# One first block of 512 tokens, another order from the third block on, and a new place for the first chunk of w_in

## The chip, the cores and the metric

The kernel runs on one core of one Trainium2 chip. The metric is the device time of one execution in microseconds. TensorE (PE) multiplies matrices, VectorE (DVE) and ScalarE (ACT) do elementwise work, GpSimd (POOL) some additions, and the queue of SyncE (SP) issues the transfers between HBM and the on-chip memory.

## What is computed

Attention with a bounded window over 4 x 768 tokens and 8 heads of 64, then two feed-forward networks:

```python
# per chunk of 32 queries: 8 memory keys, 16 keys to the left, the chunk, 8 to the right
scores = scale * (q_c @ k_full.T)
a = exp(scores - max(scores)); a = a / (sum(a) + 1e-9)
x = a @ v_full                                   # tokens x 512
h = x @ w_in                                     # 512 x 2048
g = maximum(h, 0) + alpha * minimum(h, 0)
y = g @ w_out                                    # 2048 x 512
out = ((y @ w_a) * (y @ w_b)) @ w_out2           # 512 x 1536, 512 x 1536, 1536 x 512
```

The inputs are 64-bit floats; the kernel reads them as pairs of 32-bit words.

## The kernel before

Attention works in 24 units of 128 tokens. A unit turns k and q (PE, lines 716 and 705), evacuates them, forms the scores (line 740; for the first eight units PE adds the mask, line 731), takes their maximum (DVE, line 756), the exponentials (ACT, line 766) and the normalisation (line 782), turns the probabilities P (PE, line 792) and multiplies them with v (line 806) into x32.

Products are exact to more than 16 bits by splitting: each operand is scaled by a power of two and split into a high f16 part (`split_hi`, ACT, line 347) and a low one (`split_lo`, DVE, line 351), and a product is three matmuls, high x high, high x low, low x high (`gemm3`, lines 910 to 912). The scale needs the largest value of a whole operand: a transpose on PE (line 310) and a chain of small DVE steps (lines 315 to 326).

Weights come as words. Eight chunks of w_in and eight of w_out are turned into 32-bit floats on ACT and DVE (lines 531 to 560), scaled and split. The whole of w_in has one scale, so none of its chunks can be split before all eight are in. w_in's words lie in places that are free at the start: its first chunk in xhl (later the split x), the next three in ghl, the last four where w_out's split form will be. `raw` has three places for the words of w_out and, later, of the second network's weights (`wa`, `wb`, `w3`; 18 chunks, split and spilled to HBM).

Tokens go through the first network in blocks. `first = [2, 2]` makes two blocks of 256 tokens; five of 512 follow. For each block `gemm1` forms g for 16 slices of w_in, and `gemm2` forms y for 4 slices. The two first blocks share xhl and ghl: both have their `gemm1` before the `gemm2`. From 680 us on the second network runs in six passes of 512 tokens (`second`), with the products built from seven part products; for the last pass the operands of the output product are made by `operands`: four additions over quarter blocks (`sums`, line 367, on POOL or DVE) and the splits, once the scale of the whole pass is known.

All this is written as operations with costs in microseconds (`dve`, `act`, `pe`, ...), ranks and dependencies. `Schedule.emit` plays them through on a model of the engines and issues whichever can start first; the order that results is fixed in each engine's queue. So the costs don't change what an instruction takes on the chip, only its place in the queue.

Of the kernel before, what the change touches and what calls it, by code (L numbers as in the profile page):

```python
# [13 lines left out]
ALU = mybir.AluOpType  # L14
# [157 lines left out]


def dve(n, rate=1.04, pointers=0):
    return 0.07 + 0.06 * pointers + n * rate / 1000


def act(n, pointers=0):
    return 0.06 + 0.09 * pointers + n * 0.833 / 1000

# [10 lines left out]
def tile_attention_moe_moe2(  # L191
# [15 lines left out]
    nc = tc.nc  # L207
# [11 lines left out]
    KF2 = DF2 // P  # L219
    TB = 512  # L220
    EARLY = 8
    CW = 256
    CR = 64
# [80 lines left out]
    def scale(amax, s, inv, reads, writes, rank=-2000, after=()):  # L304


        ps = Buf(mm_slots)

        def across():
            nc.tensor.transpose(out=ps.tile[:, :P], in_=amax().to_broadcast([P, P]), identity=ident)  # L310

        m = Buf(m_slots)

        def largest():
            nc.vector.tensor_reduce(out=m.tile, in_=ps.tile[:, :P], axis=AX.X, op=ALU.max)
# [12 lines left out]
        sd.op("PE", pe(P, 2), -9000, across, reads, [(ps, 0)])  # L328
        sd.op("DVE", dve(P), rank, largest, [(ps, 0)], [(m, 0)])
        sd.op("DVE", 0.07, rank, power, [], [(m, 0)])  # L330
        sd.op("DVE", 0.07, rank, inverse, [(m, 0)], [(m, 1)])
        last = [(m, 2)] if after else writes
        sd.op("DVE", 0.09, rank, itself, [(m, 1)], last)
        for i, fn in enumerate(after):
            sd.op("DVE", 0.07, rank, fn, [(m, 2 + i)], writes if i == len(after) - 1 else [(m, 3 + i)])

# [143 lines left out]
    def raw_tile(c):  # L480
        if c < 4:
            t = (in_g if c else in_x).tile.rearrange("p x k t -> p (x k t)")
            c = max(0, c - 1)
# [21 lines left out]
    def chunk(nm, c, w, kt, cw, rank, load_rank):  # L505
# [84 lines left out]
        if nm != "w1":  # L590
            sd.op("ACT", act(n, 2), rank, sizes, [fk], [rk, (key + "am", 0)])
            scale(
                lambda: am, s, inv, [(key + "am", 0)], [(key + "s", 0), (f"inv_{nm}{c}", 0)],
                rank=rank - 0.3, after=[after],
            )
# [65 lines left out]
    def attention(iu, b, u, x32, part, am, rank):  # L661
# [166 lines left out]
        sd.op(  # L828
            "PE", 0.3 + 4 * pe(KW, 4) + (0.35 if early else 0.0), prank, scores,
            [(qT, 0), (kT, 0), (kT, 1)], [(ps, 0)],  # L830
# [6 lines left out]
        sd.op("ACT", 8 * act(KW, 2) + 0.3, rank, exps, [(sm, "m")] + [(ps, 0)] * early, [(sm, 0)])  # L837
        sd.op("DVE", 0.07, rank, sums, [(sm, 0)], [(sm, 2)])
        sd.op("DVE", 0.09, rank, part_of, [], [(sm, 2)])
        for o in range(2):  # L840
            sd.op(
                None, {"DVE": dve(n), "ACT": 4 * act(KW, 1) + 0.15}, rank, lambda e, o=o: norm(e, o),
                [(sm, 2), (sm, 0)], [(sm, ("n", o))],
            )
            sd.op("PE", 4 * pe(P, 2), prank, lambda o=o: p_turn(o), [(sm, ("n", o))], [(pp, o)])
            sd.op(None, either(512), rank, lambda e, o=o: p_evac(e, o), [(pp, o)], [(pT, o)])
        sd.op("PE", 0.3 + 8 * pe(64, 4), prank, values, [(vw, 0), (pT, 0), (pT, 1)], [(px, 0)], holds=[x32])
        sd.op(None, either(512), rank, x_evac, [(px, 0)], [(x32, part)])
# [17 lines left out]
    def x_block(jb, x32, xhl, c0, rank):  # L866
# [12 lines left out]
        sd.op(  # L879
            "DVE", 0.1, rank, largest, [(x32, ("am", p0 + i)) for i in range(nu)], [(f"amx{jb}", 0)]  # L880
        )

        after = [
            lambda: nc.vector.tensor_tensor(out=s, in0=s, in1=ral, op=ALU.mult),

            lambda: nc.vector.tensor_tensor(out=iy, in0=inv, in1=iy0, op=ALU.mult),
        ]
# [72 lines left out]
    def gemm2(jb, m, ghl, c0, n, iy, rank):  # L960
# [25 lines left out]
        for i in range(4):  # L986
# [7 lines left out]
            "DVE", 0.07, rank - 1000, evac_scale,  # L994
            [(f"sx{jb}", 0)] + [(f"inv_w2{2 * m + i}", 0) for i in range(2)], [("iym", jb, m)],
        )
# [38 lines left out]
    for c in range(NR):  # L1035
        chunk("w2", c, w_out, KF1, CR, 5 + c, 4.1 + 0.5 * c)
    shared = Buf(x32_slots), Buf(xhl_slots), Buf(ghl_slots)
    place = []
    for jb in range(NB):
        if jb < len(first):  # L1040
            place.append((*shared, blocks[jb][0] * P, (-6, -3.2, -3.1, -3.0)[jb], 5 + 0.1 * jb, 8 + 0.1 * jb))
        else:
            b = jb - len(first) + 2
            ar = 9 if b == 2 else (b - 1) * 10 + 4
            place.append((Buf(x32_slots), Buf(xhl_slots), Buf(ghl_slots), 0, ar, b * 10 + 5, b * 10 + 8))
    for jb, (x32, xhl, ghl, c0, ar, r1, r2) in enumerate(place):
        n = blocks[jb][1] * P
        iy = x_block(jb, x32, xhl, c0, ar)
# [4 lines left out]
    for i, (nm, w) in enumerate((("wa", w_a), ("wb", w_b), ("w3", w_o2))):  # L1053
        for c in range(NJ):
            chunk(nm, c, w, 0, 0, 1000 + c, 1000 + c)


# [116 lines left out]

    def operands(r, b, h, s, reads, cost):

        o = Buf(s32_slots)
        unit = lambda: b.tile
        others = lambda: o.tile

        sd.op("POOL", 0.0, r, lambda: None, reads, [(h, "held")], holds=[h])
        sums(
# [16 lines left out]
    def second(jb, r):  # L1199
# [39 lines left out]

        sd.op("DVE", 0.1, r, largest_y, [(f"amy{jb}", kk) for kk in range(KK)], [(f"amy1{jb}", 0)], late=3.0)  # L1240
        after = [
# [12 lines left out]

        sd.op("DVE", 0.1, r, largest, [("amp", jb, j) for j in js], [(f"amp1{jb}", 0)], late=0.0 if last_ else 3.0)
        after = [
# [123 lines left out]
```

## Time and profile before

| | us |
|---|---|
| median of 3 runs | 1192.36 (1191.29 to 1195.16) |
| the profiled execution's own time | 1191.92 |
| its span, first to last instruction | 1190.2 |
| PE busy | 1126.7 (95%) |
| DVE busy | 868.6 (73%) |
| ACT busy | 604.7 (51%) |
| POOL busy | 226.5 (19%) |

A matmul's row gives its start and a modelled end, and the next begins before that end; so the distance of starts is what a matmul costs. [...] An idle time in brackets is that of the engine before the row, with what ended it.

### The profile page before, as it was taken

The numbers are of one execution on the slowest core, as the hardware profiler recorded it, in microseconds if no ns is written. First come the engines' busy times: TensorE is split into PE (matmuls) and PEld (weight loads), VectorE is DVE, ScalarE is ACT, GpSimd is POOL, SyncE is SP. The second block draws the span as 40 slices with busy tenths as digits, with TensorE's granted clock in tenths as the row PEclk, the third lists the DMA queues.
The fourth block names the chain that finished last, engine by engine and source line by source line (L and its number), as shares of the span: only waits on it lengthen the run. The fifth ranks groups of instructions, "written<-read, shape, count | busy, mean of one in ns | idle before, by whom it ended". The sixth has DMA issues, their size and how long they took to land.

```text
span 1190.2 us, 23137 instructions
## 1 busy us (share of the span) xinstructions
PE 1126.7 (95%) x9304; PEld 811.2 (68%) x9304; DVE 868.6 (73%) x1533; ACT 604.7 (51%) x1326; POOL 226.5 (19%) x293
## 2 busy tenths in 40 slices
PE   4399999999999999999999999999999999999988
PEld 3278886555445554444444588888888888888877
DVE  6989998987998799335243187886867958858881
ACT  4689778975886698246253032433424423324340
POOL 1000012111112212100300010242433414234130
PEclk9589999999999999899999999999999999999999
DMA  9935664647635633530103052512513514315101
GB/s 263 258 81 139 154 191 127 186 132 219 200 103 167 194 127 106 179 140 32 50 10 133 27 190 90 188 66 94 191 54 112 173 37 156 130 52 187 63 36 37
DMA packets 162523, 150.93 MB, mean 127 GB/s; under 512 B 104032, under 2 KB 139888, under 8 KB 162416
## 3 DMA queue, kind: packets, MB, share of 16 engines
q1 hardware_dynamic: 162416, 149.45, 41.5%
q8 instruction: 73, 1.20, 0.4%
q14 instruction: 34, 0.28, 0.1%
HBM read 120.33 MB, written 29.10 MB: 126 GB/s over the span
## 4 chain that ended last, share of the span: by engine, by line
PE 74%; DVE 13%; ACT 6%; DMA 3%; SPq 2%; issue 2%; ACTq 0%; DVEq 0%
PE mm L910 23%; PE mm L912 23%; PE mm L911 23%; ACT sm L766 2%; PE pair L792 2%; DVE ghl L942 1%; DVE g L933 1%; DVE w L553 1%; PE mm L806 1%; DMA qt<-in_q_dram 1%; SPq L688 1%; DVE nm L756 1%; DVE w L560 1%; ACT sp L347 1%; ACT t L930 1%
## 5 line engine op out<-in xcount | busy, mean ns | idle before, releaser
L912 PE MATMUL mm<-xhl,w 128*128 128x512 f16 (+1 forms) x448 | 157.3, 351 | 1.9 <-DVE w L553 1.9
L910 PE MATMUL mm<-xhl,w 128*128 128x512 f16 (+1 forms) x448 | 157.6, 352 | 0.3 <-ACT t L930 0.2
L912 PE MATMUL mm<-ghl,w 128*128 128x512 f16 (+1 forms) x448 | 156.9, 350 | 0.9 <-DVE w L351 0.9
L911 PE MATMUL mm<-xhl,w 128*128 128x512 f16 (+1 forms) x448 | 157.4, 351 | 0.3 <-DVE xhl L351 0.3
L910 PE MATMUL mm<-ghl,w 128*128 128x512 f16 (+1 forms) x448 | 157.2, 351 | 0.0
L911 PE MATMUL mm<-ghl,w 128*128 128x512 f16 (+1 forms) x448 | 156.9, 350 | 0.0
L910 PE MATMUL mm<-units,w1b 128*128 128x256 f16 x560 | 153.4, 274 | 0.0
L911 PE MATMUL mm<-units,w1b 128*128 128x256 f16 x560 | 153.4, 274 | 0.0
L912 PE MATMUL mm<-units,w1b 128*128 128x256 f16 x560 | 153.3, 274 | 0.0
L912 PEld LDWEIGHTS <-w 128*128 128x128 f16 x896 | 88.2, 98 | 83.5 <-DVE w L553 2.2
L910 PEld LDWEIGHTS <-w 128*128 128x128 f16 x896 | 88.5, 99 | 75.5 <-issue 0.8
L911 PEld LDWEIGHTS <-w 128*128 128x128 f16 x896 | 88.3, 99 | 73.5 <-issue 1.7
L910 PE MATMUL mm<-w2b,w1b 128*128 128x256 f16 x504 | 137.4, 273 | 0.1
L912 PE MATMUL mm<-w2b,w1b 128*128 128x256 f16 x504 | 137.4, 273 | 0.0
L911 PE MATMUL mm<-w2b,w1b 128*128 128x256 f16 x504 | 137.4, 273 | 0.0
L910 PEld LDWEIGHTS <-w1b 128*128 128x128 f16 x1064 | 104.4, 98 | 13.0 <-DMA w1b<-wb_d 0.5
L911 PEld LDWEIGHTS <-w1b 128*128 128x128 f16 x1064 | 104.4, 98 | 12.7
L912 PEld LDWEIGHTS <-w1b 128*128 128x128 f16 x1064 | 104.4, 98 | 12.2
L367 POOL TENSOR_TENSOR raw<-w 128x256 f32<-128x256 f32 x18 | 16.1, 893 | 409.7 <-ACT raw L568 248.8
L933 DVE SCALAR_TENSOR_TENSOR g<-t,columns,g 128x512 f32<-128x512 f32 (+1 forms) x112 | 75.8, 683 | 24.3 <-ACT t L930 24.2
L942 DVE TENSOR_TENSOR ghl<-g,ghl 128x512 f16<-128x512 f32 (+1 forms) x112 | 70.8, 638 | 23.8 <-ACT ghl L939 23.4
L927 ACT ACTIVATE g<-mm 128x512 f32<-128x512 f32 (+1 forms) x112 | 60.5, 547 | 50.5 <-PE mm L912 48.4
(293 smaller groups left out, 2403.5 us busy)
## 6 DMA issues: line engine op xcount, KB each, us to landing
w1b<-wa_d SPq DMA_DIRECT2D x26, 896.0 KB
w1b<-wb_d SPq DMA_DIRECT2D x26, 896.0 KB
raw<-in_moe_w_out_dram SPq DMA_DIRECT2D x8, 1024.0 KB
kw<-in_k_dram SPq DMA_DIRECT2D x40, 176.0 KB
vw<-in_v_dram SPq DMA_DIRECT2D x40, 176.0 KB
qt<-in_q_dram SPq DMA_DIRECT2D x24, 256.0 KB
raw<-in_moe_w_a_dram SPq DMA_DIRECT2D x12, 512.0 KB
raw<-in_moe_w_b_dram SPq DMA_DIRECT2D x12, 512.0 KB
```

The lines of the kernel that those rows point to most:

```text
L347: nc.scalar.activation(out=hi, in_=src, func=ACTF.Copy, scale=s)
L367: (nc.vector if e == "DVE" else nc.gpsimd).tensor_tensor(out=out_()[:, i], in0=x()[:, a], in1=y()[:, b], op=op)
L553: nc.vector.scalar_tensor_tensor(out=f, in0=lo, scalar=29, in1=f, op0=ALU.logical_shift_right, op1=ALU.bitwise_or)
L560: nc.vector.scalar_tensor_tensor(out=lo if nm == "w1" else f, in0=hi, scalar=KEEP, in1=f, op0=ALU.bitwise_and, op1=ALU.bitwise_or)
L766: nc.scalar.activation(out=sm.tile[:, o, g], in_=scored()[:, o, g], func=ACTF.Exp, bias=stat["nm"][:, i : i + 1], scale=1.0, accum_out=sta ...
L792: nc.tensor.transpose(out=heads(pp, P)[:KW, o, g], in_=sm.tile[:, o, g], identity=ident)
L910: nc.tensor.matmul(out=ps, lhsT=lh, rhs=rh, start=first and i == 0, stop=False)
L911: nc.tensor.matmul(out=ps, lhsT=lh, rhs=rl, start=False, stop=False)
L912: nc.tensor.matmul(out=ps, lhsT=ll, rhs=rh, start=False, stop=last and i == n - 1)
L927: nc.scalar.activation(out=g.tile[:, :n], in_=ps.tile[:, :n], func=ACTF.Relu, scale=E1)
L933: nc.vector.scalar_tensor_tensor(out=g.tile[:, :n], in0=t2.tile[:, :n], scalar=nal[:, m : m + 1], in1=g.tile[:, :n], op0=ALU.mult, op1=ALU ...
L942: nc.vector.tensor_tensor(out=ghl.tile[:, 1, m, d], in0=g.tile[:, :n], in1=ghl.tile[:, 0, m, d], op=ALU.subtract,)
```

## The change

One block of 512 tokens stands first instead of two of 256, so there are six blocks of 512, and the first product needs four units of attention. The costs that the planner uses become a table, `took`: `SHORT` holds the values as they were, `FULL` longer ones; from the third block on, and for the second network's weight chunks, `FULL` holds. w_in's first chunk goes to a place of `raw`, where w_out's third chunk then has to wait for it; w_out's loads get a later rank. The scale of x no longer waits for that of w_in (a factor `iy` is its own operation now), and 18 copies of a scale's reciprocal fall away. In the last pass the additions of `operands` may start as soon as a product and its size are there (`ready`) instead of after the scale, the first two operands have their additions in places of their own, and the places of the split operands are dealt in another order.

```diff
+SHORT = dict(
+    dve=0.07, act=0.06, rate=0.833, tiny=0.07, itself=0.09, part=0.09, largest=0.1,
+    exp=0.357, scaled=0.267, scores=1.16, values=2.02,
+)
+FULL = dict(
+    dve=0.15, act=0.17, rate=0.85, tiny=0.15, itself=0.16, part=0.2, largest=0.2,
+    exp=0.57, scaled=0.42, scores=0.9, values=1.15,
+)
+took = dict(SHORT)
 def dve(n, rate=1.04, pointers=0):
-    return 0.07 + 0.06 * pointers + n * rate / 1000
+    return took["dve"] + 0.06 * pointers + n * rate / 1000
...
-    in_x, in_g = Buf(xhl_slots), Buf(ghl_slots)
+    in_x, in_g = Buf(raw_slots), Buf(ghl_slots)
...
-    first = [2, 2]
+    first = [4]
...
         scale(
-            lambda: am1, s, inv, [(f"amx{jb}", 0), ("alpha", 0), ("s_w1", 0)], [(f"sx{jb}", 0)], after=after
+            lambda: am1, s, inv, [(f"amx{jb}", 0), ("alpha", 0)], [(f"sx{jb}", 0)], after=after
+        )
+        sd.op(
+            "DVE", took["tiny"], rank, lambda: nc.vector.tensor_tensor(out=iy, in0=inv, in1=iy0, op=ALU.mult),
+            [(f"sx{jb}", 0), ("s_w1", 0)], [(f"iy{jb}", 0)],
         )
...
-        chunk("w2", c, w_out, KF1, CR, 5 + c, 4.1 + 0.5 * c)
+        chunk("w2", c, w_out, KF1, CR, 5 + c, 6.1 + 0.5 * c)
...
+        took.update(SHORT if jb < EXACT else FULL)
...
-    def operands(r, b, h, s, reads, cost):
-        o = Buf(s32_slots)
+    def operands(r, b, h, s, reads, cost, ready=None, slots_=None):
+        o = Buf(slots_ or s32_slots)
...
-        sd.op("POOL", 0.0, r, lambda: None, reads, [(h, "held")], holds=[h])
+        sd.op("POOL", 0.0, r, lambda: None, reads if ready is None else ready, [(h, "held")], holds=[h])
...
-        pu = {j: Buf((ring_slots if i < 4 else yu_slots) if last_ else pu_slots) for i, j in enumerate(js)}
+        pu = {j: Buf((yu_slots if i < 2 else ring_slots) if last_ else pu_slots) for i, j in enumerate(js)}
         for j in js:
-            operands(r, ps[j], pu[j], lambda j=j: spj[:, j : j + 1], [(f"sp{jb}", 0), (ps[j], 0)], cost)
+            operands(
+                r, ps[j], pu[j], lambda j=j: spj[:, j : j + 1], [(f"sp{jb}", 0), (ps[j], 0)], cost,
+                [(ps[j], 0), ("amp", jb, j)] if last_ else None,
+                p32_slots if last_ and j in list(js)[:2] else None,
+            )
```

Lines of the changed kernel stand 12 to 23 further down: 716 becomes 728, 705 becomes 717, 740 becomes 752, 792 becomes 804, 806 becomes 818, 310 becomes 324, 351 becomes 365, 367 becomes 381, 910 becomes 925.

On PE, at the start, the queue before has unit 2's scores, the transposes for the scales of w_in and of x, unit 3's q, and then the first product:

```order
L740 MATMUL pair<-kT,qT 64x96 x16
L310 MATMUL mm<-ident,columns 128x128 x2
L705 MATMUL mm<-ident,qt 128x128 x4
L910 LDWEIGHTS w_94
L910 MATMUL mm<-xhl,w_94 128x256
```

Behind the same scores of unit 2 the changed queue goes on with attention. After w_in's scale come unit 3's q, unit 2's P, unit 3's k and unit 2's values:

```order
L752 MATMUL pair<-kT,qT 64x96 x16
L324 MATMUL mm<-ident,columns 128x128
L717 MATMUL mm<-ident,qt 128x128 x4
L804 MATMUL pair<-ident,sm 96x128 x8
L728 MATMUL pair<-ident,kw 128x96 x8
L818 MATMUL mm<-pT,vw 64x64 x16
```

Unit 3 follows in the same way, with unit 4's k and q, and the queue reaches the first product behind unit 4's scores, unit 5's q and the transposes for the scales of x and of a chunk of w_out:

```order
L752 MATMUL pair<-kT,qT 64x96 x16
L717 MATMUL mm<-ident,qt 128x128 x4
L324 MATMUL mm<-ident,columns 128x128 x2
L925 LDWEIGHTS w_94
L925 MATMUL mm<-xhl,w_94 128x512
```

So two whole units of attention have moved ahead of the first product.

On DVE, at the end, the queue before has the additions (L367, into s and xhl) and low splits (L351) of the last operands of the output product in this row:

```order
L351 SCALAR_TENSOR_TENSOR w1b<-s_13058,columns,w1b 128x768
L367 TENSOR_TENSOR s_13138<-xhl 128x256
L367 TENSOR_TENSOR xhl<-xhl 128x256
L367 TENSOR_TENSOR s_13138<-s_13138,xhl 128x256
L367 TENSOR_TENSOR s_13138<-xhl,s_13138 128x256
L351 SCALAR_TENSOR_TENSOR units<-xhl,columns,units 128x1024
L351 SCALAR_TENSOR_TENSOR units<-s_13129,columns,units 128x768
L351 SCALAR_TENSOR_TENSOR units<-xhl,columns,units 128x1024
L351 SCALAR_TENSOR_TENSOR units<-s_13138,columns,units 128x768
```

In the changed queue the last operands stand like this (L441, L447 and L429 evacuate the products of the pass before):

```order
L381 TENSOR_TENSOR s_12497<-xhl,s_12497 128x256
L441 SCALAR_TENSOR_TENSOR cb<-mm_12457,columns,cb 128x256
L381 TENSOR_TENSOR xhl<-xhl 128x256
L381 TENSOR_TENSOR s_12522<-s_12522,xhl 128x256
L365 SCALAR_TENSOR_TENSOR w1b<-xhl,columns,w1b 128x1024
L447 SCALAR_TENSOR_TENSOR cb<-mm_12501,columns,cb 128x512
L365 SCALAR_TENSOR_TENSOR w1b<-s_12497,columns,w1b 128x768
L429 SCALAR_TENSOR_TENSOR cb<-mm,columns,cb 128x256
L365 SCALAR_TENSOR_TENSOR w1b<-xhl,columns,w1b 128x1024
L365 SCALAR_TENSOR_TENSOR w1b<-s_12522,columns,w1b 128x768
```

Of twelve additions that stood on DVE behind the pass's scale, these three are left; four stand ahead of the scale, around its first step:

```order
L381 TENSOR_TENSOR s_12285<-w1b 128x256
L1321 SCALAR_TENSOR_TENSOR xhl<-cb,columns,xhl 128x1024
L381 TENSOR_TENSOR s_12285<-s_12285,w1b 128x256
L381 TENSOR_TENSOR s_12285<-w1b,s_12285 128x256
L423 SCALAR_TENSOR_TENSOR g<-mm,columns,cb 128x256
L1272 TENSOR_REDUCE columns<-columns 128x1
L381 TENSOR_TENSOR ghl<-quarters,ghl 128x256
L329 TENSOR_REDUCE m<-mm 128x1
```

The others moved to POOL, most of them ahead of the scale.

## Rows read from the trace of the kernel before

**Rows 1.** The page, busy time of each engine.

```profile
PE 1126.7 (95%) x9304; PEld 811.2 (68%) x9304; DVE 868.6 (73%) x1533; ACT 604.7 (51%) x1326; POOL 226.5 (19%) x293
```

**Rows 2.** By stretch: PE, PEld, DVE, ACT, POOL busy (instructions), PEclk, DMA share, GB/s.

```profile
0.00:61.12 61.12, 24.89 (x226) 18.33 (x227) 48.06 (x84) 34.13 (x83) 4.97 (x41) 0.74 0.96 258
40.00:60.00 20.00, 5.95 (x51) 3.77 (x48) 18.43 (x35) 13.27 (x29) 0.00 (x0) 0.50 1.00 231
61.12:182.91 121.79, 117.03 (x1295) 100.13 (x1294) 112.28 (x247) 100.09 (x289) 3.83 (x4) 0.97 0.56 138
182.91:488.31 305.40, 292.61 (x2352) 160.11 (x2350) 262.26 (x464) 232.42 (x580) 60.47 (x68) 0.99 0.54 157
478.00:484.00 6.00, 6.00 (x39) 3.14 (x40) 2.16 (x3) 1.29 (x3) 3.36 (x4) 0.51 0.72 234
1140.00:1164.00 24.00, 19.45 (x153) 15.67 (x151) 17.42 (x24) 8.73 (x10) 8.53 (x8) 0.86 0.07 25
```

**Rows 3.** PE timeline: start, us, instruction, [idle before it <- what ended it].

```profile
60.24 1.09 PE L705 MATMUL mm<-ident,qt 128*128 128x128 f32 x4 [10.33 <-DMA qt<-in_q_dram]
61.12 0.42 PE L910 MATMUL mm<-xhl,w 128*128 128x256 f16 x1
61.34 0.42 PE L911 MATMUL mm<-xhl,w 128*128 128x256 f16 x1
...
74.06 0.28 PE L912 MATMUL mm<-xhl,w 128*128 128x256 f16 x1 [1.94 <-DVE w L553]
...
78.91 0.27 PE L910 MATMUL mm<-xhl,w 128*128 128x256 f16 x1
...
85.02 0.27 PE L912 MATMUL mm<-xhl,w 128*128 128x256 f16 x1
...
269.72 0.38 PE L910 MATMUL mm<-ghl,w 128*128 128x512 f16 x1
...
277.27 0.38 PE L912 MATMUL mm<-ghl,w 128*128 128x512 f16 x1
```

**Rows 4.** PE by stretch, one attention unit's four pieces between products, and their sum.

```profile
85.13:86.66 1.53, 1.53 (x18) 1.00 0.04 11
...
sum 4.29, PE 4.29; mean PE 1.07
```

**Rows 5.** DVE by line and shape, 42.6 to 59.1: count | busy us, mean ns | idle.

```profile
L351 DVE SCALAR_TENSOR_TENSOR w<-ghl,columns,w 128x1024 f16<-128x1024 f32 x3 | 3.8, 1279 | 0.0
L560 DVE SCALAR_TENSOR_TENSOR w<-w,w 128x1024 int32<-128x1024 int32 x3 | 3.7, 1218 | 0.0
...
L351 DVE SCALAR_TENSOR_TENSOR xhl<-x,columns,xhl 128x512 f16<-128x512 f32 x2 | 1.4, 748 | 0.2 <-ACT xhl L347 0.2
...
L756 DVE TENSOR_REDUCE nm<-pair 128x8 f32<-128x768 f32 x1 | 1.0, 951 | 0.0
L546 DVE TENSOR_SCALAR w<-w 128x1024 int32<-128x1024 int32 x1 | 0.7, 685 | 0.0
```

**Rows 6.** Timeline of DVE and ACT, the splits of the first x.

```profile
57.64 1.42 DVE L351 SCALAR_TENSOR_TENSOR xhl<-x,columns,xhl 128x512 f16<-128x512 f32 x2 [0.24 <-ACT xhl L347]
...
56.90 1.32 ACT L347 ACTIVATE xhl<-x,columns 128x512 f16<-128x512 f32 x2
```

**Rows 7.** PE timeline, the last long wait of attention.

```profile
476.83 0.37 PE L806 MATMUL mm<-pT,vw 96*64 96x64 f32 x4 [2.48 <-DVE columns L815]
477.98 1.76 PE L806 MATMUL mm<-pT,vw 96*64 96x64 f32 x28 [0.78 <-DMA vw<-in_v_dram]
```

**Rows 8.** PE timeline, the waits ahead of the last pass's output products.

```profile
1156.42 0.39 PE L912 MATMUL mm<-units 128*128 128x256 f16 x1 [3.25 <-DVE units L351]
1158.54 0.39 PE L912 MATMUL mm<-units 128*128 128x256 f16 x1 [1.30 <-DVE units L351]
```

**Rows 9.** DVE's additions of line 367 in one stretch: busy us (instructions).

```profile
1133.00:1156.00 23.00, 5.89 (x12) 1.00 0.12 46
```

**Rows 10.** One of POOL's additions of line 367, whole trace: ns min/median/max.

```profile
L367 POOL TENSOR_TENSOR s<-x x13: 724/727/1705, 564.7 to 1139.6; 128x256 f32<-128x256 f32 x13
```

More of the change, by code (lines that the diff above doesn't have):

```diff
@@ L171, in pe @@
     return passes * ((n if passes != 4 else max(n, 128)) / 2400 + 0.0005)
+SHORT = dict(
[7 more added lines that the diff above has]
+took = dict(SHORT)
 def dve(n, rate=1.04, pointers=0):
-    return 0.07 + 0.06 * pointers + n * rate / 1000
+    return took["dve"] + 0.06 * pointers + n * rate / 1000
 def act(n, pointers=0):
-    return 0.06 + 0.09 * pointers + n * 0.833 / 1000
+    return took["act"] + 0.09 * pointers + n * took["rate"] / 1000
 def pool(n):
@@ L220, in tile_attention_moe_moe2 @@
     TB = 512
+    EXACT = 2
     EARLY = 8
@@ L329, in scale @@
         sd.op("DVE", dve(P), rank, largest, [(ps, 0)], [(m, 0)])
-        sd.op("DVE", 0.07, rank, power, [], [(m, 0)])
-        sd.op("DVE", 0.07, rank, inverse, [(m, 0)], [(m, 1)])
+        sd.op("DVE", took["tiny"], rank, power, [], [(m, 0)])
+        sd.op("DVE", took["tiny"], rank, inverse, [(m, 0)], [(m, 1)])
         last = [(m, 2)] if after else writes
-        sd.op("DVE", 0.09, rank, itself, [(m, 1)], last)
+        sd.op("DVE", took["itself"], rank, itself, [(m, 1)], last)
         for i, fn in enumerate(after):
-            sd.op("DVE", 0.07, rank, fn, [(m, 2 + i)], writes if i == len(after) - 1 else [(m, 3 + i)])
+            sd.op("DVE", took["tiny"], rank, fn, [(m, 2 + i)], writes if i == len(after) - 1 else [(m, 3 + i)])
     def to_float(m):
@@ L828, in attention @@
         sd.op(
-            "PE", 0.3 + 4 * pe(KW, 4) + (0.35 if early else 0.0), prank, scores,
+            "PE", took["scores"] + (0.35 if early else 0.0), prank, scores,
             [(qT, 0), (kT, 0), (kT, 1)], [(ps, 0)],
@@ L836, in attention @@
             sd.op("DVE", dve(2 * n), rank, largest, [(sm, 0)], [(sm, "m")])
-        sd.op("ACT", 8 * act(KW, 2) + 0.3, rank, exps, [(sm, "m")] + [(ps, 0)] * early, [(sm, 0)])
-        sd.op("DVE", 0.07, rank, sums, [(sm, 0)], [(sm, 2)])
-        sd.op("DVE", 0.09, rank, part_of, [], [(sm, 2)])
+        sd.op("ACT", 8 * took["exp"], rank, exps, [(sm, "m")] + [(ps, 0)] * early, [(sm, 0)])
+        sd.op("DVE", took["tiny"], rank, sums, [(sm, 0)], [(sm, 2)])
+        sd.op("DVE", took["part"], rank, part_of, [], [(sm, 2)])
         for o in range(2):
             sd.op(
-                None, {"DVE": dve(n), "ACT": 4 * act(KW, 1) + 0.15}, rank, lambda e, o=o: norm(e, o),
+                None, {"DVE": dve(n), "ACT": 4 * took["scaled"]}, rank, lambda e, o=o: norm(e, o),
                 [(sm, 2), (sm, 0)], [(sm, ("n", o))],
@@ L846, in attention @@
             sd.op(None, either(512), rank, lambda e, o=o: p_evac(e, o), [(pp, o)], [(pT, o)])
-        sd.op("PE", 0.3 + 8 * pe(64, 4), prank, values, [(vw, 0), (pT, 0), (pT, 1)], [(px, 0)], holds=[x32])
+        sd.op("PE", took["values"], prank, values, [(vw, 0), (pT, 0), (pT, 1)], [(px, 0)], holds=[x32])
         sd.op(None, either(512), rank, x_evac, [(px, 0)], [(x32, part)])
@@ L879, in x_block @@
         sd.op(
-            "DVE", 0.1, rank, largest, [(x32, ("am", p0 + i)) for i in range(nu)], [(f"amx{jb}", 0)]
+            "DVE", took["largest"], rank, largest, [(x32, ("am", p0 + i)) for i in range(nu)], [(f"amx{jb}", 0)]
         )
@@ L994, in gemm2 @@
             "DVE", 0.07, rank - 1000, evac_scale,
-            [(f"sx{jb}", 0)] + [(f"inv_w2{2 * m + i}", 0) for i in range(2)], [("iym", jb, m)],
+            [(f"iy{jb}", 0)] + [(f"inv_w2{2 * m + i}", 0) for i in range(2)], [("iym", jb, m)],
         )
@@ L1055, in tile_attention_moe_moe2 @@
             chunk(nm, c, w, 0, 0, 1000 + c, 1000 + c)
+    took.update(SHORT)
     ring_slots, yu_slots, pu_slots, w3_slots, p32_slots = (Slots(0, None) for _ in range(5))
@@ L1238, in largest_y @@
             nc.vector.tensor_reduce(out=am1y, in_=am, axis=AX.X, op=ALU.max)
-        sd.op("DVE", 0.1, r, largest_y, [(f"amy{jb}", kk) for kk in range(KK)], [(f"amy1{jb}", 0)], late=3.0)
+        sd.op("DVE", took["largest"], r, largest_y, [(f"amy{jb}", kk) for kk in range(KK)], [(f"amy1{jb}", 0)], late=3.0)
         after = [
@@ L1253, in largest @@
             nc.vector.tensor_reduce(out=am1, in_=amp, axis=AX.X, op=ALU.max)
-        sd.op("DVE", 0.1, r, largest, [("amp", jb, j) for j in js], [(f"amp1{jb}", 0)], late=0.0 if last_ else 3.0)
+        sd.op("DVE", took["largest"], r, largest, [("amp", jb, j) for j in js], [(f"amp1{jb}", 0)], late=0.0 if last_ else 3.0)
         after = [
```

19 lines of the change are left out of this document (8 added, 11 removed).

## Prediction

> **What bounds the kernel now.** I read the page's busy time first, then the engines by stage, then the PE timeline where PE is idle. On the page PE is busy for 1126.7 of 1190.2 us [rows 1]. The stages tell where it isn't [rows 2]. Up to 61.12 us, where the first product of the first matrix product starts, PE works 24.9 us and idles 36.2. While attention still runs beside the products it idles 4.8 us (to 182.9) and 12.8 us (to 488.3), together 17.6. Between 1140 and 1164 it idles 4.6. With the 3.6 us behind PE's last instruction, while the output lands, that is nearly all of the 63.5. So behind 61.12 the kernel is PE work with some 23.6 us of holes, and its end moves with three things: when the first product starts, how much PE work is left from there, and the holes.
>
> Holes cost more than their length. The first product starts at half clock: 0.22 us from one 256-column matmul to the next, against 0.109 from 78.91 to 85.02 (56 matmuls) [rows 3]. The granted clock of 0.97 from 61.12 to 182.91 [rows 2] makes 0.03 x 121.8 = 3.7 us lost; I put about half behind the start and half (1.6) behind the 1.94 us stall at 74.06 [rows 3]. After attention's last stall [rows 7] the clock is 0.51 from 478 to 484: 2.9 us lost. From 1140 to 1164 it is 0.86: 3.4 us, part of which is the hole itself [rows 2].
>
> **The start: one block of 512.** PE's queue now has units 2 and 3 of attention whole, and unit 4's scores, ahead of the first product (the PE order rows above). Up to 42.6 us both kernels' queues are the same. From there I count along DVE, busy for 18.4 of the 20 us from 40 to 60 [rows 2]. Before, 16.4 us of its time lie between 42.6 and the end of xhl's low split at 59.06 [rows 6]; then PE waits until 60.24 for a load of q that its queue has ahead of the product [rows 3]. In the changed order there stand (each instruction begins 0.07 to 0.08 before the one ahead of it ends, so I take the means of [rows 5] less that): 9 word operations and 2 maxima at 1.14 (12.5), 8 low splits of w_in at 1.20 (9.6), 6 mask steps at 0.61 (3.7), 2 row maxima at 0.87 (1.7), 4 low splits of xhl at 0.67 (2.7), and small ones that I put at 7.9 (four evacuations of kT and pT, sizes of x, reciprocals, three scales' chains). Sum 38.1: never before 80.7.
>
> To this come waits in the queue. PE is at half clock there (0.50 [rows 2]), so a unit's steps take twice what they take at full clock (1.53 us for the first stretch of [rows 4]). Step by step: 0.9 where a word step waits for ACT's first high split, 0.9 for unit 2's transposes, 0.9 for unit 3's scores, 0.6 for its pT, 2.0 for its values, 0.9 for the scale's transpose; at the end ACT's four high splits, 0.62 each [rows 6], stand ahead of the last low split, 0.5 more than DVE alone. Some hide in each other; I take 5.6. The first product starts at 42.6 + 38.1 + 5.6 = 86.3, **25.2 us later**. Bounds: 81 with no wait, 92 with twice these.
>
> What comes back: two whole units of attention no longer lie behind the start, each 4.29 us of PE at full clock [rows 4]: **8.6**. 768 matmuls of 256 columns become 384 of 512: two at 0.109 against 0.2157 (269.72 to 277.27, 35 matmuls) [rows 3], 0.0025 x 384 = **1.0**. All eight chunks of w_in are split before the product, so the stall at 74.06 has nothing left to wait for: 1.94 and the 1.6 behind it, **3.5**.
>
> Loads: w_in's first chunk now takes one of three places of raw words, so the third w_out load waits for that chunk's low split (about 56.9 in my count), and unit 4's k and q stand behind it on SP. From 40 to 60 the queue moved 231 GB/s [rows 2]; w_out's 1.05 MB and unit 4's 0.65 are 7.4 us, so some 65 us, and PE wants this k at 73: covered by 8 us. Unit 3's loads now stand ahead of w_out's and come earlier.
>
> **From the third block on.** The planner is told longer durations, so it puts P's transposes further behind their scores: mostly 48 to 72 matmuls between them where mostly 36 to 48 stood. DVE gets easier too: it is busy 112.3 of 121.8 us, then 262.3 of 305.4 [rows 2], and some 22 us of that now lie ahead of the product. I take it that the stall of 2.48 + 0.78 [rows 7] goes, with 2.8 of half clock: **6.0**. The other holes of attention are 17.6 - 1.9 - 3.3 = 12.4; I take 8 in the new order, **4.4** less. Bounds: none left, or as many as before and a new stall with half clock, 5 more.
>
> **The end.** The last block's output products wait for the low splits of their operands, 3.25 and 1.30 us [rows 8]. Before, 12 sums stand on DVE behind the scale, 5.89 us [rows 9]. Now 4 stand ahead of the scale and 3 behind it, some 1.3 us: 4.5 less. The scale's transpose stays on PE between the same products. By the changed order the last low split but one (the DVE order rows above) ends at about 1153.8 in the old time, where PE wants it at 1153.7. So the 4.55 goes to about 0.3, and 2.2 of half clock with it: **6.5**; bounds 3 and 7.
> On POOL such a sum takes 0.72 to 1.71 us [rows 10]. [...]
>
> **The sum.** 25.2 - 8.6 - 1.0 - 3.5 - 6.0 - 4.4 - 6.5 = -4.8. The profiled execution took 1191.92 us around its span of 1190.2; the median of three runs is 1192.36, 0.4 more. 1192.36 - 4.8 = 1187.6; I say **1187.5**.
>
> **Rivals.**
> (a) Slower: the late start is not paid back. DVE stays as crowded beside the products as it is (0.92 of 61 to 183 [rows 2]), since w_out's eight chunks still fall due there, and PE waits for it as often as now. Then the 3.5, 6.0 and 4.4 stay: 1187.5 + 13.9 = 1201. It decides once holes and half clock between the first product and 490 pass some 18 us. Against it are the wider distances; for it, that the order shows no durations.
> (b) Half of that: the two big stalls go, the small ones don't, or the end gives only 3: 1191 to 1195, no difference.
> (c) The order gains more: start at 82, 3 us of small holes: 1187.5 - 4 - 5 = 1178.
> (d) It doesn't do what it says: loads hold up unit 4, and each us past 73 moves the start by one. That needs them 8 us later than counted; at 13 later it would be slower, 1200.
>
> **How the numbers follow.** About 0.3%, 3.6 us, is what a measurement can tell from no change. Forecast 0.45, (a) 0.15, (b) 0.25, (c) 0.12, (d) 0.03. Below 1188.8 lie (c) and most of the forecast's own spread (start +-4, small holes +-4, end -0.5 to +3.5), 0.55; above 1195.9 lie (a) and (d) with a little of the rest, 0.17; between them 0.28. The range reaches from (c) to near (a), 1178.5 to 1200.
>
> **What would show it.** The first 512-column product at 82 to 92 us; behind it no stall on a split of w_in; less than 10 us of PE holes until 490, and full clock there but at the start; less than 1.5 us of holes in the last 50 us, at full clock. I am wrong if the start is past 92, or if one of attention's waits is over 2 us and takes the clock with it.

## The result and the profile after

The changed kernel takes 1174.61 us (median; 1173.79 to 1176.86) against 1193.76 beside it: ratio 0.9844, interval 0.982 to 0.9869, 19 us less. The forecast was 1187.5 with a range of 1178.5 to 1200; the time lies below it. The direction was right, the gain four times what the sum gave. The profiled execution took 1173.79 us, 18.1 less than the profiled one of before. One execution of the run e5 below took 4635 us in a slow state, and neither it nor its trace is used.

The page's busy times, against [rows 1]:

```profile
PE 1124.7 (96%) x8919; PEld 777.5 (66%) x8919; DVE 867.6 (74%) x1472; ACT 593.5 (51%) x1257; POOL 240.7 (21%) x298
```

PE has nearly the same work in 18 us less. By stretch, against [rows 2] (PE, PEld, DVE, ACT, POOL busy, PEclk, DMA share, GB/s; PEclk is the granted clock as a share of the full one): up to the first product; the first block's 16 slices and its output products; the rest of attention; and the last 52 us.

```profile
0.00:82.77 82.77, 44.20 (x400) 32.41 (x401) 66.97 (x110) 49.75 (x123) 4.98 (x41) 0.71 0.90 231
82.77:192.94 110.17, 107.53 (x821) 57.65 (x821) 97.09 (x186) 86.45 (x218) 8.39 (x8) 0.98 0.53 136
192.94:502.87 309.93, 309.24 (x2384) 167.26 (x2383) 254.15 (x437) 216.32 (x533) 53.61 (x56) 1.00 0.50 147
...
1120.00:1172.00 52.00, 47.81 (x437) 42.37 (x434) 26.74 (x40) 13.05 (x15) 6.04 (x5) 1.00 0.11 41
```

PE idles 2.6 us in the first block and 0.7 in the next 310 us, at full clock but for the start: PEclk is 0.51 from 82.77 to 86.3 us, where a 512-column matmul begins 0.425 after the one before (84.14 to 85.84, 4 matmuls), and 1.00 from there on to 502.87. Before it was 17.6 us in these stages. What is left of PE's waits, from 84 to 500 us (for whom PE waited: us in total, times, longest):

```profile
PE mm L324 <- ACT raw L583: 1.3, 2, 0.8
PE pair L804 <- ACT ghl L954: 0.8, 1, 0.8
PE mm L925 <- ACT t L945: 0.7, 1, 0.7
PE mm L926 <- DVE xhl L365: 0.4, 1, 0.4
```

No wait for a load or for P's normalisation is among them. The start, PE and below it DVE (start, us, instruction, idle before it):

```profile
66.39 1.12 PE L717 MATMUL mm<-ident,qt 128*128 128x128 f32 x4 [4.15 <-DMA qt<-in_q_dram]
...
80.32 0.48 PE L324 MATMUL mm<-ident,columns 128*128 128x128 f32 x1 [1.57 <-ACT raw L583]
82.77 0.58 PE L925 MATMUL mm<-xhl,w 128*128 128x512 f16 x1 [1.97 <-ACT xhl L361]
83.76 0.59 PE L926 MATMUL mm<-xhl,w 128*128 128x512 f16 x1 [0.41 <-DVE xhl L365]
```

```profile
80.97 2.73 DVE L365 SCALAR_TENSOR_TENSOR xhl<-x,columns,xhl 128x512 f16<-128x512 f32 x4
```

The first product begins 21.65 us later than before, ahead of the end of the low splits (83.70). At the end one hole is left where there were 3.25 and 1.30 [rows 8]:

```profile
1142.65 0.28 PE L927 MATMUL mm<-units,w1b 128*128 128x256 f16 x1 [0.67 <-DVE w1b L365]
```

Three stages carry the difference of the two profiled spans. The start costs 21.65. From the first product to the second network's first product the time falls from 619.06 (61.12 to 680.18) to 586.29 us (82.77 to 669.06), 32.8 less. From there to the last instruction it falls from 510.0 to 502.9, 7.1 less.

### The profile page after: what moved, and what is told of

It is laid out like the page before. It is cut to its first block, busy times and chain, and to the rows that moved or that the text cites. A ratio compares the mean times of both kernels' runs of the same rounds, so it can differ in the third digit from the quotient of the medians.

```text
span 1172.0 us, 22247 instructions
## 1 busy us (share of the span) xinstructions
PE 1124.7 (96%) x8919; PEld 777.5 (66%) x8919; DVE 867.6 (74%) x1472; ACT 593.5 (51%) x1257; POOL 240.7 (21%) x298
## 3 DMA queue, kind: packets, MB, share of 16 engines
q8 instruction: 70, 1.15, 0.4%
## 4 chain that ended last, share of the span: by engine, by line
PE 86%; DVE 7%; ACT 3%; SPq 2%; DMA 1%; issue 1%; POOL 0%; ACTq 0%; POOLq 0%
PE mm L925 26%; PE mm L926 26%; PE mm L927 26%; PE mm L818 2%; PE pair L804 2%; PE pair L752 1%; PE pair L728 1%; DVE w L568 1%; DMA w1b<-wb_d 1%; SPq L700 1%; DVE w L575 1%; PE mm L717 1%; ACT sm L778 1%; DVE w L365 1%; SPq L688 0%
## 5 line engine op out<-in xcount | busy, mean ns | idle before, releaser
L925 PE MATMUL mm<-xhl,w 128*128 128x512 f16 x384 | 146.3, 381 | 2.7 <-ACT xhl L361 2.0
L926 PE MATMUL mm<-xhl,w 128*128 128x512 f16 x384 | 146.0, 380 | 0.4 <-DVE xhl L365 0.4
L927 PE MATMUL mm<-xhl,w 128*128 128x512 f16 x384 | 146.0, 380 | 0.0
L925 PE MATMUL mm<-ghl,w 128*128 128x512 f16 x384 | 145.6, 379 | 0.0
L927 PE MATMUL mm<-ghl,w 128*128 128x512 f16 x384 | 145.5, 379 | 0.0
L926 PE MATMUL mm<-ghl,w 128*128 128x512 f16 x384 | 145.5, 379 | 0.0
L927 PEld LDWEIGHTS <-w 128*128 128x128 f16 x768 | 75.2, 98 | 91.7 <-issue 1.4
L926 PEld LDWEIGHTS <-w 128*128 128x128 f16 x768 | 75.3, 98 | 86.0 <-issue 3.9
L925 PEld LDWEIGHTS <-w 128*128 128x128 f16 x768 | 75.4, 98 | 85.2 <-issue 0.6
L927 PEld LDWEIGHTS <-w1b 128*128 128x128 f16 x1064 | 104.1, 98 | 12.8 <-DVE w1b L365 0.9
L957 DVE TENSOR_TENSOR ghl<-g,ghl 128x512 f16<-128x512 f32 x96 | 67.0, 703 | 28.3 <-ACT ghl L954 27.8
L942 ACT ACTIVATE g<-mm 128x512 f32<-128x512 f32 x96 | 57.5, 599 | 56.1 <-PE mm L927 55.7
L948 DVE SCALAR_TENSOR_TENSOR g<-t,columns,g 128x512 f32<-128x512 f32 x96 | 74.2, 777 | 12.0 <-ACT t L945 11.9
```

Of the source, the lines that this page charges most:

```text
L925: nc.tensor.matmul(out=ps, lhsT=lh, rhs=rh, start=first and i == 0, stop=False)
L926: nc.tensor.matmul(out=ps, lhsT=lh, rhs=rl, start=False, stop=False)
L927: nc.tensor.matmul(out=ps, lhsT=ll, rhs=rh, start=False, stop=last and i == n - 1)
L942: nc.scalar.activation(out=g.tile[:, :n], in_=ps.tile[:, :n], func=ACTF.Relu, scale=E1)
L948: nc.vector.scalar_tensor_tensor(out=g.tile[:, :n], in0=t2.tile[:, :n], scalar=nal[:, m : m + 1], in1=g.tile[:, :n], op0=ALU.mult, op1=ALU ...
L957: nc.vector.tensor_tensor(out=ghl.tile[:, 1, m, d], in0=g.tile[:, :n], in1=ghl.tile[:, 0, m, d], op=ALU.subtract,)
```

## Experiments

Ratios are to runs of the kernel before on the same chip, with 95% intervals; us worked out from them are for 1193. Holes are PE's idle times of over 0.05 us, counted in the PE timeline, or the length of a stretch less PE's busy time in it.

**Each part by itself.** e1 is the kernel before with only the new end (`operands` with `ready` and own places, places dealt anew):

```diff
...
+                [(ps[j], 0), ("amp", jb, j)] if last_ else None,
+                p32_slots if last_ and j in list(js)[:2] else None,
...
```

> The kernel before with only the new end: additions of the last operands ahead of the scale, two of them in places of their own, the places of the split operands dealt as in the changed kernel. Theory: the end is a part by itself. In the profiles the stretch from the second network's first product to the last instruction went from 510.0 to 502.9 us, 7.1 less, of which some 0.4 lie at 780 to 800 us and not at the end. So about 1187 us against 1193.8, the two waits of 3.25 and 1.30 gone, under 1 us of holes in the last 50. Rival: the end depends on what stands ahead of it (POOL and DVE reach it earlier in the changed kernel): then less than half comes, 1190 or more, and one wait over 1 us stays.

1185.25 us, 0.9932 (0.991 to 0.9954): 8.1 less. In its profile 6.7 lie behind the second network's first product; the first product of this execution also came 0.8 us earlier, on the same order. The hole of 0.67 is there as in the changed kernel. The end is a part by itself.

e2 is the kernel before with one block of 512, w_in's first chunk among the raw words, and w_out's later rank:

```diff
-    first = [2, 2]
+    first = [4]
...
-    in_x, in_g = Buf(xhl_slots), Buf(ghl_slots)
+    in_x, in_g = Buf(raw_slots), Buf(ghl_slots)
...
-        chunk("w2", c, w_out, KF1, CR, 5 + c, 4.1 + 0.5 * c)
+        chunk("w2", c, w_out, KF1, CR, 5 + c, 6.1 + 0.5 * c)
```

> The kernel before with only the one first block of 512, w_in's first chunk among the raw words and w_out's later load rank; short durations throughout and the old end. Theory A, the longer durations take attention's holes away: the start costs 21.7 as in the profile, 8.6 for two units, 1.0 for columns and 3.5 for the stall on w_in come back, the holes behind 100 us stay at some 15 us: 1193.8 + 8.6 = 1202 us. Rival B, the one block takes the holes away by itself, since attention and its weights have run two units further ahead: under 5 us of holes between the first product and 500, and no half clock there: 1182 us. Rival C, half each: 1190 to 1195.

1206.2 us, 1.0107 (1.0083 to 1.013): 12.8 more. The first product is at 83.57, and PE's holes from there to the second network grow to 21.9 us (17.5 before). Theory A, and somewhat worse: the one block with its place and rank is a loss, and together they take no hole away. Place and rank alone (e15 below) cost 5 of these 12.8 us and have 24.7 us of holes; so beside e15 the block costs some 8 us and takes about 3 us of holes away.

e3 is the changed kernel with the old durations everywhere:

```diff
-    EXACT = 2
+    EXACT = 99
```

> The changed kernel with the short durations in every block. Theory A: the holes of the blocks from the third on come back. Before, PE had 10 us of them from 300 to 484, with 2.9 of half clock, and each costs about 0.2 more than it shows: about 1188 us. Rival B, the one block did it: 1175, with under 5 us of holes until 500. Between them (C): 1180, if only the long waits at 474 come back.

1196.58 us, 1.0023 (1.001 to 1.0036). The table of durations alone is worth 0.0179, 21 us. Theory A, with some 9 us more than it expected. PE's stretch, beside it that of the changed kernel, and e3's main waits from 84 to 500 us:

```profile
200.00:500.00 300.00, 283.12 (x2236) 153.04 (x2235) 247.82 (x420) 227.93 (x563) 60.33 (x63) 0.99 0.52 153
```

```profile
200.00:500.00 300.00, 299.31 (x2329) 161.92 (x2324) 245.93 (x422) 210.46 (x524) 53.61 (x56) 1.00 0.50 144
```

```profile
PE mm L324 <- ACT raw L583: 9.1, 9, 2.6
PE pair L804 <- ACT sp L361: 2.9, 1, 2.9
PE mm L818 <- DMA vw<-in_v_dram: 2.2, 2, 1.2
```

Nearly half of it is PE's transpose for a weight chunk's scale (L324), standing ahead of products in the queue and waiting for ACT's pass over the chunk. DVE is as busy as in the changed kernel over the same 300 us (247.8 against 245.9); so it isn't room on DVE that was missing, and e11 below says the same of ACT. What is left is the place of the instructions in the queues.

No run isolates x's freed scale and the 18 fallen copies. e2 and e1 add up to 0.0039 over the kernel before, and e3, which has these two besides, is at 0.0023; so with one block they are worth some 2 us, which the noise covers.

e4 keeps the durations and the freed scale of x, and undoes the rest: e2's three edits the other way round, and the end.

```diff
-    first = [4]
+    first = [2, 2]
...
-    in_x, in_g = Buf(raw_slots), Buf(ghl_slots)
+    in_x, in_g = Buf(xhl_slots), Buf(ghl_slots)
...
-        chunk("w2", c, w_out, KF1, CR, 5 + c, 6.1 + 0.5 * c)
+        chunk("w2", c, w_out, KF1, CR, 5 + c, 4.1 + 0.5 * c)
...
-                [(ps[j], 0), ("amp", jb, j)] if last_ else None,
-                p32_slots if last_ and j in list(js)[:2] else None,
```

> The changed kernel with two first blocks of 256, w_in's first chunk in xhl's place, w_out's old load rank and the old end. What is left of the change are the longer durations from the third block (here from token 512) on, x's scale freed of w_in's, and the copies that fell away. Theory A: the holes behind 183 us, 12.8 us with 2.9 of half clock and 0.2 a hole for 15 holes, go but for 1 or 2 us: 1193.8 - 17 = 1177 us; the start and its stall of 1.94 stay as before. Rival B: the order by itself does little, the holes stay above 10 us: 1190 to 1194.

1192.87 us, 0.9996 (0.9983 to 1.0009): nothing. But its stretches tell two things:

```profile
59.95:200.00 140.05, 122.11 (x1350) 104.53 (x1350) 123.68 (x257) 106.93 (x304) 3.66 (x4) 0.92 0.52 129
200.00:500.00 300.00, 297.41 (x2315) 162.28 (x2314) 246.83 (x419) 209.56 (x522) 53.96 (x56) 1.00 0.49 143
```

Behind 200 us the holes have gone (2.6 us; 12.8 before). Ahead of it they have grown to 18, with new long waits:

```profile
181.42 0.47 PE L324 MATMUL mm<-ident,columns 128*128 128x128 f32 x1 [5.41 <-ACT raw L582]
185.72 1.09 PE L803 MATMUL pair<-ident,sm 128*96 128x128 f32 x4 [3.82 <-DVE sm L793]
```

The third block here begins at token 512, in the changed kernel at 1024. So units planned long stand beside w_out's chunks, which are planned short; the next runs ask whether that is the reason.

**Where the longer durations may begin.** e5 and e9 are one kernel, run twice: e4 with the new end, and the table from token 1024 on:

```diff
-    EXACT = 2
+    EXACT = 3
...
+                [(ps[j], 0), ("amp", jb, j)] if last_ else None,
+                p32_slots if last_ and j in list(js)[:2] else None,
```

> The changed kernel with two first blocks of 256, w_in's first chunk in xhl's place and w_out's old load rank, the new end kept, and the longer durations from token 1024 on, as in the changed kernel (there from the third block; here from the fourth). Theory: the longer durations work only where they don't stand beside w_out's chunks, which are planned with the short ones; from token 1024 on they take the holes away whatever the start. Then this kernel has the changed one's holes behind 300 us (under 1 us), the end of it, and the earlier start of before: 1174.6 - 21.7 + 8.6 + 1.0 + 3.5 + 1.7 (holes of 61 to 183 as before) = 1168 us. Rival: the one block is needed, since only it puts attention two units further ahead: over 10 us of holes behind 183 and 1180 us or more.

> The kernel with two first blocks of 256, the longer durations from token 1024 on and the new end once more, for its trace. Its time was 1169.2, 5.4 below the changed kernel. Theory: the first product at 60 to 62 us, the stall on w_in near 72 us and the small holes until 183 us as before, under 1 us of holes from 300 to 490, one hole of about 0.7 at the end. Rival: the two blocks keep their holes until 490 and gain elsewhere.

1169.17 us both times; 0.9793 (0.9774 to 0.9812) and 0.9809 (0.9792 to 0.9827). In the trace of e9 the first product is at 59.41, the holes until 200 are 7.3 us, those from 200 to 500 0.5. The table takes the holes behind 200 us away whatever the start, and the one block isn't needed for it; without it the kernel is 4 to 6 us faster than the changed one (0.0035 and 0.0051).

e6 lets the table begin at token 512 in the changed kernel, e7 does so and plans w_out's chunks long too (its second added line):

```diff
-    EXACT = 2
+    EXACT = 1
...
+    took.update(FULL)
     for c in range(NR):
         chunk("w2", c, w_out, KF1, CR, 5 + c, 6.1 + 0.5 * c)
```

> The changed kernel with the longer durations from the second block (token 512) on instead of the third, which is where they began in the kernel with two first blocks that gained nothing. Theory: attention planned long beside w_out's chunks planned short makes PE wait for the sizes of w_out, as it did there (3.18, 5.41 and 3.82 us between 133 and 186): some 9 us of holes between 85 and 200, 1184 us. Rival: with one first block it doesn't matter where they begin: 1174 to 1177.

> The longer durations from the second block on, and for w_out's chunks too. Theory: what hurts is the mix; with w_out's chunks planned as long as attention, PE's transposes for their scales stand behind the sizes again, and the waits on them between 85 and 200 are under 2 us together: 1174 us. Rival: DVE and ACT have no room beside the first products whatever the order, and the waits only change their place: 1182 or more.

e6: 1179.54 us, 0.9881 (0.9864 to 0.9898), 4 us more than the changed kernel, with new waits of 1.84 (from 163.6 us) and 2.65 (from 180.9). e7: 1180.95 us, 0.9894 (0.9875 to 0.9914), with one of 6.07 (from 180.8) and a first product at 85.4. Where the table begins matters, by 4 us with one block and by some 16 with two (e5 is 24 below e4, 8 of it for the new end). But planning w_out's chunks long does not mend it, so the mix of the two tables beside w_out's chunks is not the cause; why that stretch wants the short values stays open.

e10 is e9 with w_in's first chunk among the raw words and w_out's later rank:

```diff
-    in_x, in_g = Buf(xhl_slots), Buf(ghl_slots)
+    in_x, in_g = Buf(raw_slots), Buf(ghl_slots)
...
-        chunk("w2", c, w_out, KF1, CR, 5 + c, 4.1 + 0.5 * c)
+        chunk("w2", c, w_out, KF1, CR, 5 + c, 6.1 + 0.5 * c)
```

> The same with w_in's first chunk among the raw words and w_out's later load rank, as in the changed kernel. It tells what place and rank are worth by themselves. Theory: they are needed only where the first block splits w_in before its product; here the third load of w_out waits longer and nothing else: 1169 to 1172 us. Rival: w_out's later loads leave the queue to attention's, and the first product's wait for them goes: 1165 us.

1162.92 us, 0.9758 (0.9741 to 0.9776), the fastest of all, 29 us below the kernel before. My theory was wrong: place and rank are worth 6 us here. The first product comes only 0.8 us earlier. But in the trace it no longer stands behind a wait of 9.59 us for x's split (e9); PE waits 3.29 and 2.98 and has attention work behind them. The stall near 72 us is 1.23, for another cause, and no hole is left from 200 to 500:

```profile
56.46 1.06 PE L804 MATMUL pair<-ident,sm 128*96 128x128 f32 x4 [2.98 <-DVE sm L794]
57.31 1.49 PE L728 MATMUL pair<-ident,kw 96*128 96x96 f32 x8
58.59 0.42 PE L925 MATMUL mm<-xhl,w 128*128 128x256 f16 x1
```

```profile
200.00:500.00 300.00, 300.00 (x2343) 163.10 (x2342) 247.66 (x426) 211.40 (x522) 48.23 (x56) 1.00 0.51 146
```

More than half of the 6 us is the granted clock. From the first product to 110 us, e9 and below it e10:

```profile
59.41:110.00 50.59, 45.47 (x462) 37.94 (x462) 46.42 (x99) 45.22 (x133) 0.00 (x0) 0.91 0.51 116
58.59:110.00 51.41, 48.73 (x559) 41.99 (x560) 48.80 (x103) 48.56 (x145) 0.00 (x0) 0.98 0.54 124
```

By estimate half clock costs 0.09 x 50.6 = 4.6 us in e9 and 0.02 x 51.4 = 1.0 in e10.

e15 makes the edits of that same diff alone on the kernel before:

> The kernel before with only w_in's first chunk among the raw words and w_out's later load rank: two blocks of 256, short durations, old end. With the longer durations these two gave 6.2 us (1169.2 to 1162.9), 0.8 at the first product, the rest in the stall near 72 us and the waits up to 100. Theory: they work at the start, whatever the durations behind it: 1186 us against 1192. Rival: with the short durations the w_out chunks only wait elsewhere: 1190 or more.

1196.92 us, 1.0042 (1.0026 to 1.0059): 5 us more, though its first product came at 57.3, 3.8 us earlier. Its holes from there to the second network are 24.7 us (17.5 before), 15.1 of them ended by ACT. The granted clock from the first product to 110 us is 0.85, where it was 0.94. So the earlier start is given back behind it. That the durations decide between this loss and e10's gain is not shown: e9 and e10 also have x's freed scale and the new end, which e15 has not, and no run separates these.

**Which durations.** The table makes DVE's and ACT's steps longer, but PE's scores and values shorter (1.16 to 0.9, 2.02 to 1.15). e8, e11, e13 and e14 are the changed kernel with a part of the table, e12 with more:

```diff
 # e8
+FULL = dict(SHORT, act=0.17, rate=0.85, exp=0.57, scaled=0.42)
 # e11
+FULL = dict(SHORT, dve=0.15, tiny=0.15, itself=0.16, part=0.2, largest=0.2, scores=0.9, values=1.15)
 # e12
+FULL = dict(
+    dve=0.23, act=0.28, rate=0.85, tiny=0.23, itself=0.23, part=0.3, largest=0.3,
+    exp=0.78, scaled=0.57, scores=0.9, values=1.15,
+)
 # e13
+FULL = dict(SHORT, scores=0.9, values=1.15)
 # e14
+FULL = dict(SHORT, dve=0.15, tiny=0.15, itself=0.16, part=0.2, largest=0.2)
```

> The changed kernel, in which only ACT's durations are the longer ones (its fixed part and rate, exponentials, scaled copies); DVE's steps and PE's scores and values are planned as before. With all short, 20 us of holes came back, about 14 of them ended by ACT (sizes of weight chunks, casts, splits), the rest by DVE or a load. Theory: ACT's durations alone bring most of it: 1180 us, holes ended by ACT under 3 us. Rival: the longer DVE steps hold attention back, which frees both engines: 1190 us or more.

> The changed kernel with the other half of the table: DVE's steps and PE's scores and values as in the changed kernel, ACT's durations short. All short costs 22.0 us, ACT's part alone gave 11.5 of them back. Theory: the parts add up, each engine's own margin takes away the waits on that engine: about 1186 us, with the holes ended by ACT left. Rival: either part holds attention back for both engines: 1181 us or less.

> The changed kernel with durations longer by once more about the same step (ACT's fixed part 0.28, DVE's 0.23, an exponential 0.78, a scaled copy 0.57). The traced distance of two exponentials is 0.36 us, the short value; the longer value is about the sum of the two records (0.37 and 0.20) that overlap. Theory: the longer values act as a margin, and more of it neither helps nor hurts, since only 3.3 us of holes are left until 500: 1173 to 1177 us. Rival: they work because they are what a result takes to be there; beyond that attention falls behind and the blocks wait for their x: 1180 us or more.

> The changed kernel, in which the second set of durations differs from the first in PE's two entries alone: scores 0.9 instead of 1.16, values 1.15 instead of 2.02, which are shorter and close to the trace (0.82 and 1.08 from start to start). Theory P: planned too long by 1.28 us a unit, over the 16 units that the table covers 20 us, PE comes to its products and transposes that much before the plan and waits there; right durations are enough: 1173 to 1177 us. Rival D, the longer DVE steps give the room: 1188 us or more.

> The changed kernel, in which the second set differs in DVE's entries alone (0.08 longer a step, near the length of a DVE record; the distance of two steps is the short value). Theory P: little, PE still comes early: 1188 us or more. Rival D: 1173 to 1178.

| table | us | ratio | holes 200 to 500 |
|---|---|---|---|
| all short (e3) | 1196.58 | 1.0023 (1.001 to 1.0036) | 16.8 |
| ACT's (e8) | 1185.07 | 0.993 (0.9914 to 0.9946) | 8.2 |
| DVE's (e14) | 1185.64 | 0.9953 (0.9936 to 0.997) | 9.4 |
| PE's two (e13) | 1180.43 | 0.9908 (0.9889 to 0.9927) | 4.0 |
| DVE's and PE's (e11) | 1172.9 | 0.9844 (0.9826 to 0.9862) | 0.2 |
| all (changed kernel) | 1174.61 | 0.9844 (0.982 to 0.9869) | 0.7 |
| longer still (e12) | 1173.88 | 0.985 (0.9832 to 0.9868) | 0.2 |

Against all short, ACT's entries give 11 us, DVE's 8, PE's 14: together 33, where the whole table gives 21. So the parts don't add, and DVE's with PE's are enough. The theories of e8 and e11 both fell (I had thought each engine's entries mend its own waits); e11's rival came. Of e13 and e14 neither theory was right: PE's two are the largest part, but not the whole. e12 shows that once 0.7 us are left, more margin does nothing.

How a part works is only half shown. In the last 16 units P's transposes stand on average 61.5 products behind their scores in the changed kernel, 54.8 in e8 and 54.0 in e11, against 49.5 in e3. But in e14 and e13 the distance is 48.8 and 48.0, and 7.4 and 12.8 us of the holes went all the same. The largest part of it is the waits of weight chunks' transposes for ACT's pass (L324 in e3): 9.1 us with all short, 5.1 in e14, 3.3 in e13. By which places PE's two entries do that stays open.

The costs do one thing more than the section on the kernel says: they also choose the engine of what DVE and ACT can both do (evacuations, the normalisation). In e3 ACT is busy 227.93 us from 200 to 500, in the changed kernel 210.46. This isn't the cause either, for e11 has no holes with ACT nearly as busy as in e3:

```profile
200.00:500.00 300.00, 299.81 (x2279) 161.51 (x2278) 251.45 (x435) 224.43 (x560) 56.19 (x64) 1.00 0.52 153
```

PE's entries are the ones in which the plan was wrong. One unit's values and scores in the changed kernel (PE timeline; the next row begins where the piece is through):

```profile
475.25 1.15 PE L818 MATMUL mm<-pT,vw 96*64 96x64 f32 x32
476.33 0.89 PE L752 MATMUL pair<-kT,qT 64*64 64x96 f32 x32
477.16 0.39 PE L925 MATMUL mm<-ghl,w 128*128 128x512 f16 x1
```

1.08 and 0.83 us, where the old table had 2.02 and 1.16: the plan was 1.27 a unit too long. By my reading PE came that much ahead of the plan to what stands behind them. For 16 units this makes 20 us, of which e13 gave 14; the mechanism itself no run shows.

e16 is e10 with e11's table, DVE's and PE's entries alone:

> Two first blocks of 256, new place and later loads, the new end, and DVE's and PE's entries alone from token 1024 on. Theory: the parts add, ACT's entries give nothing beside them: 1161 to 1163 us. Rival: here ACT's waits come back: 1167 us or more.

1166.19 us, 0.9784 (0.9767 to 0.9801): between the two. With two blocks ACT's entries may still be worth some 3 us (the two intervals just overlap), and e10 stays the best.

## The prediction, step by step

**What bounds the kernel**: right. PE's work behind the first product, the start and the holes account for the whole difference; DVE's load never became the bound, and rival (a) did not come.

**The start** (25.2 later, measured 21.65 in the profiles): the mechanism was right, each term a little high. DVE's work from 42.6 us to the end of the low splits is 37.6 us (38.1 said), its idle time in it 3.5 (5.6 said), and the first product goes ahead with the high splits, 0.9 us before the last low split is through, where I had put it behind. PE waits 4.15 us for unit 4's q, which lands at 66.4 us; I had counted its loads to 65. DVE had work all that time (busy 4.15 of the 4.15 us from 62.24 to 66.39), so by my reading this costs nothing, and it is far from the 8 us that rival (d) needed.

**What comes back**: the two units (8.6), the columns (1.0) and the stall on w_in with its half clock (3.5) came about as said: without holes (0.16 us more for each, as below) and half clock, PE's time between the first products of the two networks falls by some 10.5 us, where 9.6 were said for units and columns, and no wait on a split of w_in is left in the rows. That these terms and the start together are a loss is what e2 shows, which has the old end and the short durations: 12.8 us, where 25.2 - 8.6 - 1.0 - 3.5 = 12.1. (The two agree by luck in part: the start was cheaper and the holes grew.)

**From the third block on**: this is the step that failed. I gave the order 6.0 for the long stall and 4.4 of 12.4 us for the small holes, 10.4 in all; the table is worth 21 us (e3). Three things were wrong. First, I took the rest of the small holes to be there anyway (8 us); 3.3 are left, of them 0.7 behind 200 us. Second, I wrote that the planner is told longer durations, here and in the section on the change, and passed over the two that became shorter, which alone give 14 us (e13). Third, I priced a hole by its bracket. At full clock a product's row ends 0.27 us (256 columns) or 0.38 (512) after its start, but the next would start after 0.109 or 0.2157 [rows 3]; so by these rows a hole behind a product costs 0.16 more than its bracket. In the kernel before:

```profile
71.85 0.27 PE L911 MATMUL mm<-xhl,w 128*128 128x256 f16 x1
```

From there to 74.06 [rows 3] are 2.21 us, 2.10 more than 0.109, where the bracket says 1.94. Until the second network the kernel before had 26 holes over 0.05 us, the changed one has 6: twenty fewer, by estimate 20 x 0.16 = 3.2 us that stand in no bracket. Between the first product and the second network the prediction gave 23.5 us back, measured were 32.8. Of the 9.3 between them the holes make 4.7 and these 3.2; of the last 1.4, some 0.4 are half clock, which the changed kernel has only until 86.3 us (0.51 from 82.77 to there, 1.00 behind it), and 1.0 stays unexplained.

There is a further point that the sum could not show: its parts are not independent. With short durations place and rank made the holes worse by 7 us (e15 against before), and the block took 3 of them away again (e2).

**The end** (6.5; measured 7.1 in the profiles and 8.1, with an interval of 5.5 to 10.7, in e1): right. One hole of 0.67 is left, at full clock (PEclk 1.00 from 1120 to 1172). Behind the scale POOL makes five additions for the last operands, between 1132 and 1140 us, of 0.72 to 1.71 us, three of them over 1.3, as in [rows 10]. Each of these three ran beside a low split on DVE (that of 1.32 us for its first 0.73, that of 1.71 for its first 1.11), the two of 0.72 beside none; and of DVE's three additions there the one beside POOL took 0.94 us, the other two 0.41. That one engine lengthened the other's work there is not shown: no run separates them. The wait behind the long additions is the 0.67 and no more.

**The rivals**: (c) had the start (82) and the small holes (3) as they came, but only 0.12 of the chance; its 1178 was still 3 us too high, about the price of a hole above. What would have made the range right is (c) with none of the small holes left, a bound that I named, and that price: 1187.5 - 4 - 8 - 3.2 = 1172.

## What to carry to other kernels

Where a planner's table sets the order, compare its entries with the trace in both directions: two pieces that were planned too long cost 14 us here. Where the entries were right, longer ones gave 8 and 11 us all the same, so a margin is worth a run. Price a hole in a pipelined stream from start to start, not by the bracket. And test an edit to the start and an edit to the order together as well as apart: place and rank cost 5 us in the old kernel and gained 6 in the new one.

## What was not expected of the hardware

In these traces records of one engine overlap, so a record is longer than what the instruction costs in a row. On ACT an exponential's two records are 0.37 and 0.19 us, yet the next exponential begins 0.36 after it; on DVE a 512-column step has 0.69 and the next begins after 0.61 (both from the changed kernel):

```profile
340.26 0.37 ACT L778 ACTIVATE sm<-sm,nm 128x96 f32<-128x96 f32 x1
340.52 0.19 ACT L778 ACTIVATION_READ_ACCUMULATOR sm<-sm,nm 128x1 f32 x1
340.62 0.36 ACT L778 ACTIVATE sm<-sm,nm 128x96 f32<-128x96 f32 x1
```

```profile
428.84 0.69 DVE L957 TENSOR_TENSOR ghl<-g,ghl 128x512 f16<-128x512 f32 x1
429.45 0.75 DVE L948 SCALAR_TENSOR_TENSOR g<-t,columns,g 128x512 f32<-128x512 f32 x1
```

The old entries are these distances (0.357; 0.07 + 512 x 1.04 / 1000 = 0.60), the new ones the records (0.57 for the two of an exponential; 0.15 + 0.53 = 0.68). So the old entries were right about what these two steps need in a row, the changed ones overstate it, and they still order better.
